# Reordering the first weight loads of a decode kernel by row length, and the query product with them

## The chip, the cores and the metric

One core of one Trainium2 chip. The time is the device time of one execution in microseconds; a kernel's time is the median of several runs. The span in a profile is the part between the first and the last instruction, some 2 us less. PE, DVE, ACT, POOL and SP are the core's TensorE, VectorE, ScalarE, GpSimd and SyncE; "PEclk" is the TensorE clock that was granted. A load runs on 16 DMA engines at once, and a row is one contiguous run of a load for one partition: the piece that one DMA engine moves in one record.

## The reference, cut to what matters

```python
# x: (8, 1, 448) bf16;  k_cache, v_cache: (8, 8, 4096, 256), the last W = 1024 positions are used
# wq: (448, 4096);  wo: (4096, 448);  w1: (448, 1792);  w2: (1792, 448)
q = (x @ wq).reshape(B, Sq, 16, 256).transpose(0, 2, 1, 3)
# k, v: the positions used, each head repeated for two heads of q
scores = einsum("bhqd,bhkd->bhqk", q, k) * 256 ** -0.5
a = einsum("bhqk,bhkd->bhqd", softmax(scores), v)...reshape(B, Sq, 4096) @ wo
b = gelu(layernorm(x) @ w1 + b1) @ w2 + b2
g = sigmoid((x * gate_w).sum(-1))
out = g * a + (1 - g) * b
```

Every weight and every cached key and value is read once: 77.7 MB for little arithmetic.

## The kernel before

All large inputs come through one stream of loads on one queue (SP), into a ring of nine slots of 16 KB per partition. `pump` issues loads as long as slots are free; `done` frees one. A `rows_loader` issues one load per piece, and a piece's row length is the length of one contiguous run per partition. The 448 rows of wq are three blocks of 128 (r = 0, 1, 2) and a tail of 64, cut into two halves so that it fills 128 partitions.

```python
wq_m = A_wq[0:DM, :].rearrange("(p r) n -> p (r n)", r=NR)          # 128 x 12288, HD = 4096
wq_t = A_wq[DM:D, :].rearrange("r (h n) -> (r h) n", h=2)           # 128 x 2048
add(("wq", 0), rows_loader([wq_m[:, 0 : 2 * HD]]))                  # 16 KB rows
add(("wq", 1), rows_loader([wq_m[:, 2 * HD : 3 * HD], wq_t]))       # 8 KB, then 4 KB rows
add_kv("k", A_k_cache, 0)                                           # 16 KB rows
add(("w1",), rows_loader([w1_m, w1_t]))
add(("w2",), rows_loader([w2_v]))
# ... keys and values in turn, then wo
pump()
nc.scalar.dma_start(x_sb[:], xf)          # four small loads on the ACT queue: x, gate, b2, b1
# ... gate_w broadcast, b2, b1
# ... constants; nc.gpsimd.memset(qw[:], 0.0), 4.4 us on POOL
def query():
    for r in range(NR + 1):
        w, o = slot("wq", r // 2), (r % 2) * HD
        for n in range(W // QN):
            for t in range(QUAD):
                # ... half, c: which half of the tail, which column
                nc.tensor.matmul(Sq[32 * t : 32 * t + NB, n * QN : (n + 1) * QN],
                                 lhsT=xT[:, r + half, :], rhs=w[:, o + c : o + c + QN],
                                 start=(r == 0), stop=(r == NR), skip_group_check=True)
    done(2)
# norm_and_gate(); query(); then keys, scores, values ...
```

## Time and profile before

| | before |
|---|---|
| time, median of 3 runs (lowest to highest) | 190.34 us (189.83 to 190.40) |
| span of the profiled run | 188.2 us |
| HBM read | 77.68 MB, 413 GB/s over the span |
| stream's rate between 24 and 180 us | 430 GB/s |
| PE / DVE / ACT busy | 70% / 67% / 24% |

No engine is at its limit, but the load stream is. So what counts is when the stream begins to flow, whether it ever pauses, and when the last of its 16 DMA engines is done.

### The profile page before, as it was taken

Reading aid. Unit: us, or ns where it says so; the run is one execution under the profiler, and the core shown is the slowest. Engines: PE = TensorE matmul, PEld = TensorE weight load, DVE = VectorE, ACT = ScalarE, POOL = GpSimd, SP = SyncE. Lnnn points to the kernel's source line nnn. Section 1 sums busy time; section 2 is a strip of 40 time slices with the busy share of each in tenths; the row PEclk is TensorE's granted clock in tenths of the full one; section 3 lists DMA queues with packets and bytes.
Section 4 is the critical chain, followed back from the end, with each engine's and each line's share of the span. In section 5 each row is a group of like instructions: output and inputs, shape, how many; then the busy total and the mean of one; then the engine's idle time right before and its main releaser. Section 6 shows DMA issues by size and latency. Waiting matters only on the chain.

```text
span 188.2 us, 2351 instructions
## 1 busy us (share of the span) xinstructions
PE 132.2 (70%) x938; PEld 68.0 (36%) x950; DVE 126.7 (67%) x177; ACT 45.4 (24%) x93; POOL 6.7 (4%) x15
## 2 busy tenths in 40 slices
PE   0017969998857986666957597849385969698974
PEld 0012853344425342422433153324142424245452
DVE  3960478999949494949494949595867767695300
ACT  3032310134040404040404031404040313125300
POOL 8500000000000000000000000000000000000000
PEclk9999756999997599996999789999999999999999
DMA  6999999999999999999999999999999999999991
GB/s 210 417 435 428 436 425 426 432 432 432 428 428 435 428 435 428 428 432 428 432 437 425 421 439 435 421 432 439 425 425 435 439 428 425 425 442 432 409 392 38
DMA packets 6396, 77.83 MB, mean 413 GB/s; under 512 B 857, under 2 KB 1138, under 8 KB 1778
## 3 DMA queue, kind: packets, MB, share of 16 engines
q1 hardware_dynamic: 6208, 77.67, 97.1%
q8 instruction: 7, 0.11, 0.2%
q10 hardware_dynamic: 178, 0.02, 0.1%
q14 instruction: 3, 0.02, 0.0%
HBM read 77.68 MB, written 0.01 MB: 413 GB/s over the span
## 4 chain that ended last, share of the span: by engine, by line
DMA 76%; DVE 15%; PE 4%; ACT 2%; issue 1%; DVEq 0%; ACTq 0%; SPq 0%
DMA slot<-in_A_k_cache_dram 40%; DMA slot<-in_A_v_cache_dram 20%; DMA slot<-in_A_wo_dram 15%; DVE kt L344 7%; DMA x_sb<-in_A_x_dram 2%; PE Sq L358 2%; DVE xz L243 1%; ACT qw L399 1%; DVE mx L428 1%; DVE qw L401 1%; ACT qs L368 1%; PE A_lo L662 0%; PE qp L386 0%; PE qt L373 0%; DVE ET L458 0%
## 5 line engine op out<-in xcount | busy, mean ns | idle before, releaser
L344 DVE STREAM_TRANSPOSE kt<-slot 128x2048 int32<-128x2048 int32 x32 | 73.7, 2306 | 31.8 <-DMA slot<-in_A_k_cache_dram 31.8
L416 PE MATMUL S<-kt,qw 128*128 128x512 bf16 x256 | 66.0, 402 | 31.0 <-DVE kt L344 28.5
L416 PEld LDWEIGHTS <-qw 128*128 128x128 bf16 x256 | 25.6, 100 | 66.3 <-issue 43.9
L521 ACT ACTIVATE oT<-fin,gg_s 128x16 bf16<-128x16 f32 x16 | 5.2, 328 | 75.0 <-PE fin L518 75.0
L445 ACT ACTIVATE E<-S,nmx 128x1024 bf16<-128x1024 f32 x16 | 22.2, 1389 | 1.9 <-DVE nmx L442 1.9
L428 DVE TENSOR_REDUCE mx<-S 128x1 f32<-128x1024 f32 x16 | 19.0, 1186 | 0.0
L488 PE MATMUL PO<-slot,ET 128*16 128x512 bf16 x256 | 17.5, 395 | 0.3 <-DMA slot<-in_A_v_cache_dram 0.3
L497 ACT ACTIVATE first<-PO,own 128x256 f32<-128x256 f32 x16 | 7.6, 474 | 27.0 <-PE PO L488 27.0
L458 DVE STREAM_TRANSPOSE ET<-E 128x512 int32<-128x512 int32 x16 | 11.2, 698 | 2.2 <-ACT E L445 2.2
L436 PE MATMUL mz<-m,same 128*128 128x4 f32 x32 | 6.2, 265 | 5.7 <-ACT oT L521 5.4
L410 PE MATMUL S<-place,foreign 128*128 128x512 bf16 x25 | 9.8, 390 | 0.1
L436 PEld LDWEIGHTS mz<-m,same 128*128 128x128 f32 x32 | 5.0, 195 | 7.5 <-ACT oT L521 6.6
L469 PEld LDWEIGHTS den<-rowsum,rowden 128*128 128x128 f32 x32 | 6.4, 206 | 3.1 <-issue 0.8
L488 PEld LDWEIGHTS <-ET 128*16 128x16 bf16 x256 | 5.1, 89 | 4.9 <-issue 1.0
L410 PEld LDWEIGHTS <-foreign 128*128 128x128 bf16 x32 | 3.2, 99 | 8.6 <-issue 6.9
L480 ACT ACTIVATE rsel<-sel,rb 128x8 f32<-128x8 f32 x16 | 4.7, 292 | 1.0 <-DVE rb L479 1.0
L469 PE MATMUL den<-rowsum,rowden 128*128 128x1 f32 x32 | 4.9, 222 | 0.0
L401 DVE CAST qw<-qp 32x512 bf16<-32x512 f32 x4 | 2.7, 686 | 3.1 <-ACT qw L399 3.1
L662 PE MATMUL A_lo<-slot,oP 128*8 128x224 bf16 x32 | 3.7, 258 | 1.2 <-DMA slot<-in_A_wo_dram 1.1
L290 POOL MEMSET qw<- 128x5120 bf16 x1 | 4.4, 4355 | 0.0
L593 PEld LDWEIGHTS <-foreign 128*128 128x128 bf16 x33 | 2.9, 99 | 3.6 <-issue 0.8
L593 PE MATMUL idle<-place,foreign 128*128 128x512 bf16 x16 | 4.1, 378 | 0.1
(144 smaller groups left out, 99.4 us busy)
## 6 DMA issues: line engine op xcount, KB each, us to landing
slot<-in_A_k_cache_dram SPq DMA_DIRECT2D x16, 2048.0 KB, 38.8
slot<-in_A_v_cache_dram SPq DMA_DIRECT2D x16, 2048.0 KB, 36.9
slot<-in_A_wo_dram SPq DMA_DIRECT2D x3, 896.0 KB, 30.9
slot<-in_A_wq_dram SPq DMA_DIRECT2D x1, 2048.0 KB, 7.5
slot<-in_B_w_dram SPq DMA_DIRECT2D x1, 1568.0 KB
slot<-in_B_w_dram SPq DMA_DIRECT2D x1, 1344.0 KB, 11.8
slot<-in_A_wq_dram SPq DMA_DIRECT2D x1, 1024.0 KB, 9.5
slot<-in_A_wo_dram SPq DMA_DIRECT2D x1, 672.0 KB, 27.7
```

What stands on the lines that cost most here:

```text
L344: nc.vector.transpose(kt[:].rearrange("p c k x r -> p (c k x r)").bitcast(WORD), kn[:, hf * CH * Dh : (hf + 1) * CH * Dh].bitcast(WORD),)
L410: nc.tensor.matmul(S[u][:, cols], lhsT=foreign[:], rhs=place[:], start=True, stop=False)
L416: nc.tensor.matmul(S[u][:, cols], lhsT=qw[:, j, u, m * RQ : m * RQ + P], rhs=kt[:, :, k, :, par], start=False, stop=(k == NK - 1 and par = ...
L428: nc.vector.reduce_max(mx[:], S[u][:], axis=AXIS.X)
L436: nc.tensor.matmul(mz[:], lhsT=same[:], rhs=m4[:], start=True, stop=True)
L445: nc.scalar.activation(E[:].rearrange("p c x i -> p c i x"), S.pop(u)[:].rearrange("p (c i x) -> p c i x", i=PAIR, x=BLK), ACT.Exp, bias=n ...
L458: nc.vector.transpose(ET[:].rearrange("p c r i -> p (c r i)").bitcast(WORD), E[:].rearrange("p c x i -> p (c x i)").bitcast(WORD),)
L469: nc.tensor.matmul(den[u][:], lhsT=rowden[:], rhs=rowsum[:], start=True, stop=True)
L488: nc.tensor.matmul(PO[32 * t : 32 * t + PAIR * RQ], lhsT=ET[:, c, 0:RQ, :], rhs=vn[:, PAIR * c * Dh : PAIR * (c + 1) * Dh], start=(c < QUA ...
L497: nc.scalar.activation(first[:], PO[:, 0, :], ACT.Copy, scale=own[:, 0:1])
L521: nc.scalar.activation(oT[:, half * RQ : (half + 1) * RQ, :, b].rearrange("p h j -> p j h"), sm[:], ACT.Copy, scale=gg_s[:, b : b + 1],)
L593: nc.tensor.matmul(dst, lhsT=foreign[:], rhs=place[:], start=True, stop=True)
```

## The change

Its intent is to begin the stream with short rows, so that the first data is through sooner, and to let the product take its row blocks in the order in which they land.

```diff
-    add(("wq", 0), rows_loader([wq_m[:, 0 : 2 * HD]]))
-    add(("wq", 1), rows_loader([wq_m[:, 2 * HD : 3 * HD], wq_t]))
+    add(("wq", 0), rows_loader([wq_t, wq_m[:, 0:HD]]))
+    add(("wq", 1), rows_loader([wq_m[:, HD : 3 * HD]]))
@@ query()
-        for r in range(NR + 1):
-            w, o = slot("wq", r // 2), (r % 2) * HD
+        for r in (NR, *range(NR)):
+            w = slot("wq", 0 if r in (NR, 0) else 1)
+            o = {NR: 0, 0: HH, 1: 0, 2: HD}[r]
@@ matmul
-                        start=(r == 0),
-                        stop=(r == NR),
+                        start=(r == NR),
+                        stop=(r == NR - 1),
```

(HH is 2048: the tail fills the first 2048 columns of the first slot, and block 0 follows.)

## The prediction

> **What bounds the kernel now.** I read the page's busy rows and its chain first, then the first microseconds of the DMA stream, the stretches of the run, the queue's waits and the timeline around the query product.
>
> The page, parts 2 and 4 (40 slices of 4.7 us; DMA in tenths, below it GB/s; then the chain's shares):
>
> ```profile
> DMA  6999999999999999999999999999999999999991
> GB/s 210 417 435 428 436 425 426 432 432 432 428 428 435 428 435 428 428 432 428 432 437 425 421 439 435 421 432 439 425 425 435 439 428 425 425 442 432 409 392 38
> HBM read 77.68 MB, written 0.01 MB: 413 GB/s over the span
> DMA 76%; DVE 15%; PE 4%; ACT 2%; issue 1%; DVEq 0%; ACTq 0%; SPq 0%
> ```
>
> The load stream is full from the second slice to the last but one, at about 430 GB/s. The engines have room (PE 70%, DVE 67%). The kernel is one queue of 77.7 MB, and its time is start of the stream, plus bytes over rate, plus a tail. The chain's end (start, length, what) fixes the tail:
>
> ```profile
> 119.99 36.94 DMA slot<-in_A_v_cache_dram
> 156.95 27.70 DMA slot<-in_A_wo_dram
> 184.65 0.04 issue
> ```
>
> The last load lands at 184.65, and the last products, two copies and the store bring the span to 188.2: 3.55 us that the change doesn't touch.
>
> The stretches of the run (us, then the engines' busy times, PE clock, DMA share, GB/s) show the beginning and the end of the stream:
>
> ```profile
> 1.50:2.00 0.50, 0.00 (x0) 0.00 (x0) 0.44 (x2) 0.50 (x1) 0.50 (x5) 1.00 1.78 360
> 2.00:2.50 0.50, 0.00 (x0) 0.00 (x0) 0.48 (x1) 0.22 (x2) 0.50 (x3) 1.00 0.55 98
> 2.50:3.00 0.50, 0.00 (x0) 0.00 (x0) 0.00 (x0) 0.00 (x0) 0.50 (x2) 1.00 0.24 100
> 3.00:3.50 0.50, 0.00 (x0) 0.00 (x0) 0.00 (x0) 0.00 (x0) 0.50 (x1) 1.00 1.00 406
> 24.00:180.00 156.00, 118.28 (x762) 58.72 (x774) 114.98 (x137) 39.06 (x83) 0.00 (x0) 0.93 1.01 430
> 183.00:184.00 1.00, 0.91 (x17) 0.69 (x17) 0.00 (x0) 0.00 (x0) 0.00 (x0) 1.00 0.58 233
> 184.00:185.00 1.00, 0.88 (x12) 0.45 (x12) 0.00 (x0) 0.00 (x0) 0.00 (x0) 1.00 0.21 81
> ```
>
> A record's bytes are booked where it starts, so the first rows, which are long, look like a burst and then a hole. The DMA records one by one tell it better. The first 16 rows, one to each of 16 engines and 16 KB each, start at 1.78 to 2.14 us (two of them at 2.58 and 2.72) and end between 2.91 and 3.60, 3.24 on average. Fourteen took 1.04 to 1.69 us, the two late ones 0.62 and 0.61, and any later 16 KB row takes 0.611. The excess of the first 16 is 0.63 us per engine. From there on no engine pauses. At the other end the share falls through 183 and 184: the engines don't finish together.
>
> The sum closes. Completions of successive 2 MB loads are 4.862 us apart, or 431 GB/s. After the first rows (0.26 of 77.67 MB) there are 77.41 MB, 179.5 us; 3.24 + 179.5 = 182.7 for the average engine. The last is 2.0 us later (184.7), since an instruction fetch of 16 KB holds up the one engine it falls on: the 16 completions of one load lie 0.53 us apart before the fetch at 24.4 us, and 1.77 us from then on.
>
> The SP queue's waits and the timeline round the query product:
>
> ```profile
> SPq L133 <- DMA slot<-in_A_wq_dram: 5.3, 1, 5.3
> 4.58 2.51 DVE L243 COPY xz<-x_sb 8x64 bf16<-8x64 bf16 x2 [2.10 <-DMA x_sb<-in_A_x_dram]
> 13.64 0.56 PE L333 MATMUL gp<-each 8*128 8x8 f32 x2 [1.63 <-DVE each L331]
> 14.13 3.51 PE L358 MATMUL Sq<-slot,xT 128*8 128x512 bf16 x32
> ```
>
> The fifth load (w1) isn't issued until the first (wq) has landed, at 8.23 us. The 32 query products begin right after the gate's little product, in program order on PE, without a wait for weights: the last of wq lands at 11.6 in the DMA records, 2.5 us before.
>
> **What the Trainium skill says.** "DMA: Bandwidth & Descriptors", section "Queues, rings and completion order", says that each DMA engine takes turns between the queues it has work for, a packet at a time. The trace agrees: x_sb's 896-byte rows, on the ACT queue, start at 2.90 to 3.49 us, each as a first 16 KB row ends. The same page, "Bandwidth" (its measured table), has the rate fall for small transfers. Within this stream the row length matters little: 4 KB rows take 0.159 us (412 GB/s over 16 engines), 8 KB rows 0.309 (424), 16 KB rows 0.611 (429). "Latency and other measured facts" on that page gives an HBM access 0.2 us on average and up to 2 us under load; the first rows' excess of 0.63 us lies between, but no view tells whether it is that. "PSUM — Partial Sum Buffer", "PSUM: the matmul accumulator", says that the first matmul of a group clears the written marks of its bank and quadrants and the rest accumulate. The diff moves start and stop with the order, so the product is the same sum in another order; no trace line bears on that.
>
> **The change part by part.**
> 1. Loads. The same 3.5 MB of wq in three loads before and after: 16, 8, 4 KB rows become 4, 8, 16 KB. No instruction and no byte is added or taken away. In the stream the cost is a sum over rows, 8 per engine of each kind (8 x 0.159 + 8 x 0.309 + 8 x 0.611 = 8.63 us), and doesn't depend on the order: 0.
> 2. The first rows. What changes is which rows meet the slow start. If the start is a fixed delay before data flows (0.63 us of it, then the line rate), the first 4 KB row ends earlier and the next follows: the same bytes by the same time, 0. If the excess is in proportion to the row (a long row has to be in before it goes out, which would be twice 0.61, close to the mean of 1.24 us), a quarter of it is left and 0.63 x 3/4 = 0.47 us is gained. If each engine gets just one row through before some point near 3 us, 12 KB less per engine is through by then, and 12/16 x 0.611 = 0.46 us is lost.
> 3. Issue. The first load is 512 KB instead of 2 MB. It lands after some 8 x 0.159 = 1.3 us of stream, at about 4 us instead of 7.9, so w1 is issued at about 4.2 instead of 8.23. The queue then holds more, but it held over 5 MB (some 13 us) at that moment already and never ran dry: 0.
> 4. x_sb. Its rows now wait for 4 KB rows instead of 16 KB ones, so it can land 0.4 to 0.9 us earlier than 4.48. But the two copies that follow (2.51 us for 8x64, where the like pair for y takes 0.29) end at 7.09, just after POOL's long memset at 7.01, and I expect them to end there again. The query product stays at 14.1, and if it came earlier, it is under the stream: 0.
> 5. The query product. 32 matmuls in another order, the same 3.5 us. Its last weights (16 KB rows now) land at 11.3 to 11.6, still 2.5 us ahead of PE: 0.
> Sum: 0, plus what the first rows do, between -0.47 and +0.46 us.
>
> **The rivals.** *The fixed delay* (nothing comes of it, 190.3): for it speaks that the two engines that began late took a normal 0.61 us and ended along with the others, as if all had waited for one moment. *The excess scales with the row* (189.9): for it speaks the factor of two, and that somebody made the change; against it the same two late engines. *The loss of one row's worth* (190.8): nothing speaks for it but that a start with short rows has less in flight. A fourth way is **the spread of the engines**: the end is set by the engine that an instruction fetch hit, and the order in which the engines begin (0.53 us apart) may fall otherwise, up to 0.3 us either way. That a new wait for weights appears in front of the query product would need 2.5 us, and even then the keys' slots are freed far ahead of the stream (a key load is issued at 38.31 and lands at 74.17).
>
> **Range and chances.** I give 0.5 to the fixed delay, 0.38 to the scaling, 0.12 to the loss: 0.38 x -0.47 + 0.12 x 0.46 = -0.12 us, so 190.2 us. The range takes the scaled gain with 0.2 us of spread at one end (189.5) and the loss with less at the other (190.8); the runs of the kernel before already lie 0.57 apart. Two per cent are 3.8 us, more than all that happens before the stream's first data: within 2% has 0.98.
>
> **What would show it.** Right: DMA share and GB/s as before from the second slice on; w1 issued near 4.2; the query product at 14.1 with no wait for a slot; wo landing within 0.5 us of 184.65. Which case it is, the average end of the first MB or so tells: level with before (fixed), 0.4 to 0.5 earlier (scaled) or later (loss). Wrong: a hole in the DMA share after 3 us, a rate of the first 3.5 MB off 8.6 us by more than 0.2, or the query product behind a wait for weights.

## The result, and the profile after

The changed kernel took 190.31 us (190.25 to 190.32, 4 runs) beside 190.22 us (189.83 to 190.40, 4 runs) of the kernel before: a ratio of 1.0007 with a 95% interval of 0.9990 to 1.0025. It is the same time. Ratios here are the mean time of one kernel's fast runs over that of the other's of the same rounds, so not quite the ratio of the medians quoted.

One kernel's runs lie some 0.5 us apart, about as far as the predicted cases lie from each other, so the time alone can't tell these apart; the traces have to.

The page after (parts 2 and 4: DMA busy tenths, GB/s, HBM total, the chain's shares):

```profile
DMA  5999999999999999999999999999999999999991
GB/s 205 411 438 416 426 434 430 428 431 435 428 424 435 438 428 424 431 435 431 424 433 435 428 424 435 431 435 424 431 431 431 428 435 431 428 424 435 413 394 42
HBM read 77.68 MB, written 0.01 MB: 412 GB/s over the span
DMA 76%; DVE 16%; PE 4%; ACT 2%; issue 1%; DVEq 0%; ACTq 0%; SPq 0%
```

The same picture: first slice 205 instead of 210 GB/s, full stream behind it. The end of the chain (start, length, what) after:

```profile
120.44 36.86 DMA slot<-in_A_v_cache_dram
157.30 0.02 issue
157.32 27.52 DMA slot<-in_A_wo_dram
```

The last load lands at 157.32 + 27.52 = 184.84 us, 0.19 later than the 184.65 of before. The stretches after (busy times, PE clock, DMA share, GB/s; a record counts where it starts):

```profile
1.50:2.00 0.50, 0.00 (x0) 0.00 (x0) 0.45 (x2) 0.50 (x1) 0.50 (x5) 1.00 0.54 106
2.00:2.50 0.50, 0.00 (x0) 0.00 (x0) 0.48 (x1) 0.21 (x2) 0.50 (x3) 1.00 0.67 221
2.50:3.00 0.50, 0.00 (x0) 0.00 (x0) 0.00 (x0) 0.00 (x0) 0.50 (x2) 1.00 0.75 216
3.00:3.50 0.50, 0.00 (x0) 0.00 (x0) 0.00 (x0) 0.00 (x0) 0.50 (x1) 1.00 1.09 372
24.00:180.00 156.00, 119.25 (x753) 58.79 (x765) 115.25 (x137) 38.97 (x83) 0.00 (x0) 0.92 1.01 430
```

The middle of the run is as before, 430 GB/s. The start isn't: with short rows a record is booked near where it runs, so the 216 GB/s at 2.5 to 3 us are real. This half microsecond is where the story lies. The queue and the product after (waits: engine, line, for whom, total, times, longest; then the timeline):

```profile
SPq L133 <- DMA slot<-in_A_wq_dram: 3.6, 2, 1.9
4.02 3.08 DVE L243 COPY xz<-x_sb 8x64 bf16<-8x64 bf16 x2 [1.54 <-DMA x_sb<-in_A_x_dram]
4.72 2.85 SPq L133 DMA_DIRECT2D slot<-in_B_w_dram  x3
13.65 0.56 PE L333 MATMUL gp<-each 8*128 8x8 f32 x2 [1.62 <-DVE each L331]
14.14 3.58 PE L359 MATMUL Sq<-slot,xT 128*8 128x512 bf16 x32
```

x lands 0.52 us earlier (3.96 instead of 4.48), its copies stretch from 2.51 to 3.08 us and end at 7.10 as before, w1 is issued at 4.72 instead of 8.23, and the product begins at 14.14 instead of 14.13.

**Looking closer at the start.** For the first microseconds I took the trace's DMA records one by one, spread each row's bytes evenly over its time and cut records at the edges of a stretch. "Occupied" below is the mean share of the 16 DMA engines that have a record running, those of small loads included (it can come out a little over 1, as records overlap slightly); "excess" is what rows took over the usual time of their length (0.159, 0.309, 0.611 us for 4, 8, 16 KB), summed and divided by 16.

| trace | first row ends (mean) | occupied 2.5 to 3 us | 0.5 MB through at | 1 MB | 4 MB | excess, 4 to 12 us |
|---|---|---|---|---|---|---|
| before | 3.24 us | 0.96 | 3.84 us | 5.02 us | 12.11 us | 0.00 us |
| after | 2.22 us | 0.63 | 3.78 us | 5.04 us | 12.33 us | 0.26 us |

The short rows do what they were meant to do: an engine's first row is through a whole microsecond earlier. Then, over half a microsecond, a third of the engines on average have nothing running. 1 MB is through at the same time as before, and later, while rows of 8 and 16 KB run, many take longer than usual, which puts the stream 0.2 us behind.

The hole has a sharp form. From some 2.4 to 2.8 us on, only about eight engines run rows of the stream (8.2 on average), for 0.3 to 0.6 us. This is so in each of the five traces below that have short rows and load x at once. x has eight rows of 896 bytes. In three of the five the eight others stand idle before the first row of x begins (in the second trace of the changed kernel from 2.62 us, with x's rows from 2.90). So they aren't busy with x: it looks as if each waited for its one row of x. The records don't name their engine, so that last step isn't shown.

### The profile page after: what moved, and what is told of

Same layout as the page of the kernel before. It is cut to its first block, busy times and chain, and to the rows that moved or that the text cites. A ratio compares the mean times of both kernels' runs of the same rounds, so it can differ in the third digit from the quotient of the medians.

```text
span 188.4 us, 2351 instructions
## 1 busy us (share of the span) xinstructions
PE 133.6 (71%) x938; PEld 68.4 (36%) x950; DVE 127.5 (68%) x177; ACT 45.4 (24%) x93; POOL 6.7 (4%) x15
## 4 chain that ended last, share of the span: by engine, by line
DMA 76%; DVE 16%; PE 4%; ACT 2%; issue 1%; DVEq 0%; ACTq 0%; SPq 0%
DMA slot<-in_A_k_cache_dram 40%; DMA slot<-in_A_v_cache_dram 20%; DMA slot<-in_A_wo_dram 15%; DVE kt L344 7%; PE Sq L359 2%; DVE xz L243 2%; DMA x_sb<-in_A_x_dram 2%; ACT qw L400 1%; DVE mx L429 1%; DVE qw L402 1%; ACT qs L369 1%; PE A_lo L663 0%; PE qp L387 0%; PE qt L374 0%; DVE ET L459 0%
## 5 line engine op out<-in xcount | busy, mean ns | idle before, releaser
L417 PE MATMUL S<-kt,qw 128*128 128x512 bf16 x256 | 67.4, 408 | 30.0 <-DVE kt L344 27.7
L443 DVE TENSOR_REDUCE nmx<-mz 128x1 f32<-128x4 f32 x16 | 2.3, 146 | 3.8 <-PE mz L437 3.7
```

The costliest lines, as they stand in the source:

```text
L417: nc.tensor.matmul(S[u][:, cols], lhsT=qw[:, j, u, m * RQ : m * RQ + P], rhs=kt[:, :, k, :, par], start=False, stop=(k == NK - 1 and par = ...
```

## The experiments

**A null, and the change again.** Both kernels unchanged, five rounds each, for the noise and for second traces.

> The kernel before, unchanged, as a null and for a second trace of the start. Time ratio 1.000 within 0.2%. If the slow start of the first 16 rows is a property of the kernel, it is there again: 14 of 16 rows over 1 us, none slow after 4 us, about 3.96 MB of the stream through at 12 us. If it is chance of the one trace, the number at 12 us moves by 0.1 MB or more.

> The changed kernel again. Theory A (short rows get data through earlier but the engines then run short between 2.5 and 3.2 us, and rows of 3.5 to 10 us are slower than usual): again a DMA share near 0.5 to 0.7 there, about 3.86 MB through at 12 us, last load 0.2 to 0.3 us later than in the kernel before, ratio 1.001. Theory B (chance of one trace): the bytes at 12 us lie within 0.03 MB of those of the kernel before and the slow rows between 4 and 10 us are gone; ratio 1.000.

The kernel before against itself: 190.36 us (189.92 to 190.45), ratio 1.0001 (0.9990 to 1.0013). The changed kernel again: 190.40 us (190.00 to 190.48), ratio 1.0006 (0.9993 to 1.0018). One kernel's runs lie 0.5 us apart, so a difference of 0.1 us can't be had from times. The traces are steadier. The null's reads 0.99 occupied at 2.5 to 3 us, 1 MB at 5.03, 4 MB at 12.12, no excess; the change's 0.62, 4.98, 12.26 and 0.25 us. The hole's line of the second trace:

```profile
2.50:3.00 0.50, 0.00 (x0) 0.00 (x0) 0.00 (x0) 0.00 (x0) 0.50 (x2) 1.00 0.56 214
```

The early row, the hole and the slow rows belong to the kernel and aren't chance (theory A). One part of theory A failed: the last load was to land 0.2 to 0.3 us later than in the kernel before, and in this pair it landed 0.1 us earlier (184.68 against 184.78 us).

**Which half of the change.** `loads_only` takes the new loads with the product's old order, `order_only` the old loads with the new order.

```diff
 # loads_only, against the changed kernel
-        for r in (NR, *range(NR)):
+        for r in range(NR + 1):
-                        start=(r == NR),
-                        stop=(r == NR - 1),
+                        start=(r == 0),
+                        stop=(r == NR),
 # order_only, against the kernel before
-        for r in range(NR + 1):
+        for r in (NR, *range(NR)):
-                        start=(r == 0),
-                        stop=(r == NR),
+                        start=(r == NR),
+                        stop=(r == NR - 1),
```

> The new order of the loads with the product in its old order. Both theories: as the changed kernel within 0.1%, with the query product at 14.1 us. If the order of the product mattered, this would differ from the changed kernel by over 0.15%.

> The old loads with the product taking the tail first. The tail lands at 11.6 us and the product starts at 14.1, so no wait: as the kernel before within 0.1%, query product at 14.1 us, and the start of the stream as in the kernel before.

`loads_only`: 190.30 us, ratio 1.0004 (0.9992 to 1.0016); `order_only`: 190.48 us, ratio 1.0008 (0.9996 to 1.0020). The product starts at 14.14 and 14.13 us. The start of the stream goes with the loads alone: 0.68 occupied, 4 MB at 12.14 us and 0.22 us excess in the first, 1.00, 12.11 and 0.01 in the second. The order of the product does nothing that shows. Until the product begins, `loads_only` is the same program as the changed kernel, so its start is a third trace of it: the lag at 4 MB is then 0.22, 0.14 and 0.03 us, which is how far it scatters.

**Where the rows lie in HBM.** In the change the 16 KB rows come from blocks 1 and 2 instead of 0 and 1. Here the kernel before reads them from there, in its old order of lengths.

```diff
-    add(("wq", 0), rows_loader([wq_m[:, 0 : 2 * HD]]))
-    add(("wq", 1), rows_loader([wq_m[:, 2 * HD : 3 * HD], wq_t]))
+    add(("wq", 0), rows_loader([wq_m[:, HD : 3 * HD]]))
+    add(("wq", 1), rows_loader([wq_m[:, 0:HD], wq_t]))
@@ query()
-            w, o = slot("wq", r // 2), (r % 2) * HD
+            w = slot("wq", 1 if r in (NR, 0) else 0)
+            o = {NR: HD, 0: 0, 1: 0, 2: HD}[r]
```

> The kernel before with its 16 KB rows taken from the second and third row blocks of wq (as in the changed kernel) and its 8 KB rows from the first; the order 16, 8, 4 KB stays. If where the 16 KB rows lie in HBM makes them slow, an excess of 100 ns or more per engine shows after 4 us (0 to 7 in the three traces of the old order). If the order of lengths does, it stays under 20 ns, with first rows at 1.2 to 1.3 us and 3.95 MB through at 12 us. Time within 0.3%.

190.26 us, ratio 1.0004 (0.9989 to 1.0019); 0.98 occupied, 4 MB at 12.12 us, excess 0.01 us. The place of the rows isn't it.

**When w1 and the rest are issued.** In the change the fifth load is issued at 4.72 us instead of 8.23. Here the changed kernel's first pump stops after three slots, and the rest is issued after POOL's long memset.

```diff
-        while len(slots) < min(len(plan), consumed[0] + RING):
+        while len(slots) < min(len(plan), consumed[0] + depth[0]):   # depth = [3] at first
+    def w1_late(t):
+        nc.gpsimd.memset(t[:, 0:16], 0.0)
+        rows_loader([w1_m, w1_t])(t)
-    add(("w1",), rows_loader([w1_m, w1_t]))
+    add(("w1",), w1_late)
     nc.gpsimd.memset(qw[:], 0.0)
+    depth[0] = RING
+    pump()
```

> The changed kernel with the loads of w1 and all behind it issued not from 4.3 us on but after POOL's long memset, near 7.3 us and later. If the early issue is what slows rows between 4 and 12 us, the excess there falls from 217 to 256 ns per engine to under 100 and what is left lies after 7 us, and 3.93 MB or more is through at 12 us. If the cause is the rows themselves or the small loads, it stays at 200 or more. Time within 0.3%.

w1 is issued at 7.16 us. 190.47 us, ratio 1.0015 (0.9999 to 1.0031); 0.64 occupied, 4 MB at 12.28 us, excess 0.18 us. It fell from 0.25 but not under 0.1: the early issue isn't the cause, or not most of it.

**The small loads, first try.** The four small loads of the ACT queue were moved behind POOL's long memset, in both kernels. To make ACT wait I gave it two new tiles of 4 bytes per partition to copy. The memset ends 0.87 us earlier in this place, so the small loads are issued from 6.21 us on.

```diff
-    nc.scalar.dma_start(x_sb[:], xf)     # and gate, b2, b1
+    flag = consts.tile([NB, 1], F32)
+    flag2 = consts.tile([NB, 1], F32)
+    nc.gpsimd.memset(qw[:], 0.0)         # moved up: runs at 1.78 us on POOL instead of 2.65
+    nc.gpsimd.memset(flag[:], 0.0)
+    nc.scalar.copy(flag2[:], flag[:])
+    nc.scalar.dma_start(x_sb[:], xf)     # and gate, b2, b1
```

> The changed kernel with the four small loads of the ACT queue (x, gate, biases) issued only after POOL's long memset, near 7 us, so that nothing but the 4 KB and 8 KB rows is in the stream before. If the hole at 2.5 to 3 us (share 0.62 to 0.68 in three traces) comes from those small loads taking turns, the share there goes to 0.95 or more and 0.66 MB or more is through at 4 us (0.59 to 0.65 now). If it comes from the supply of row descriptors of the stream itself, the share stays at 0.7 or less. The slow rows of 4 to 12 us (217 to 256 ns in excess per engine) should go below 50 ns if b1's 28-byte packets cause them. The query product starts near 17 us; time within 0.3%.

> The same edit to the kernel before. If the small loads cause the slow first 16 KB rows (1.22 to 1.29 us on average instead of 0.61), these fall to under 0.8 us and the bytes through at 4 us rise from 0.56 to over 0.60 MB. If the slow start is the stream's own, first rows stay over 1.1 us. Time within 0.3%.

The start answered: 1.02 occupied at 2.5 to 3 us in the changed kernel, while the first rows of the kernel before still took 1.23 us. But both kernels came out slower, 191.33 us (ratio 1.0060, 1.0043 to 1.0078) and 191.77 us (1.0084, 1.0067 to 1.0100), which no theory of the start allowed for. The DMA records have each 2 MB load 4.894 to 4.895 us after the one before it, for the whole run, where all runs so far have 4.862. Loads that end before 18 us hardly do that at 100 us. The edit's own tiles may: they are allocated before the slots and push them up in their partition, by 64 bytes as I count it (no view shows addresses). So I tried the shift by itself and the edit without it.

**The slots' address.** The kernel before with its padding tile 64 bytes longer.

```diff
-    consts.tile([P, 112], BF16, name="pad")
+    consts.tile([P, 144], BF16, name="pad")
```

> The kernel before with its padding tile 64 bytes longer, so that all slots start 64 bytes later in each partition, and nothing else. If the slots' address caused the slower loads of the two shifted runs, each 2 MB load takes 4.893 to 4.899 us and the time is 0.5 to 0.7% up (32 such loads and the rest by 0.033 us per 2 MB: about 1.2 us). If it was the late small loads, 4.862 us and ratio 1.000.

191.56 us, ratio 1.0075 (1.0062 to 1.0088), 4.894 us per 2 MB load. The stretch of the shifted kernel that answers to the one of before:

```profile
24.00:180.00 156.00, 122.69 (x742) 59.78 (x752) 115.14 (x137) 38.68 (x82) 0.00 (x0) 0.89 1.01 427
```

427 instead of 430 GB/s, or 0.7%, and the time is 1.40 us up, a little more than the 1.2 expected. It is the stream's own rows that slow down: between 30 and 150 us a 16 KB row takes 0.6157 us on average instead of 0.6119. Everything behind the padding tile moved, not the slots alone, but no other tile is written by these rows. The first two small-loads runs have the same slow rows (0.6159 us) and aren't used for times.

**The small loads, second try.** The same without new tiles: ACT copies a piece of the memset tile into `rstd`, which is overwritten later anyway. No tile is added, so slots are back at their address.

```diff
-    nc.scalar.dma_start(x_sb[:], xf)     # and gate, b2, b1
+    nc.gpsimd.memset(qw[:], 0.0)         # moved up as before
+    nc.scalar.copy(rstd[:], qw[0:NB, 0, 0, 0:1])
+    nc.scalar.dma_start(x_sb[:], xf)     # and gate, b2, b1
```

> The same edit as the first late-small-loads run of the changed kernel, but without the two new tiles that had shifted the slots by 64 bytes. If the shift caused the 0.6% there, each 2 MB load takes 4.862 us again (4.893 to 4.899 with the shift). Start as there: share 0.95 or more at 2.5 to 3 us, 0.66 MB or more through at 4 us and 4.0 MB or more at 12 us. If the hole was what ate the gain of the short rows, the last load lands 0.1 to 0.3 us before that of the same edit on the kernel before; ratio 0.9975 to 1.000. If an engine's fetch of instructions sets the end whatever the start, no difference is seen beyond the noise of 0.15%.

> The same on the kernel before: first rows still over 1.1 us, 0.56 MB through at 4 us and 3.95 MB at 12 us, 4.862 us per 2 MB load, ratio 0.999 to 1.001.

Stretches of the changed kernel with late small loads:

```profile
2.50:3.00 0.50, 0.00 (x0) 0.00 (x0) 0.00 (x0) 0.00 (x0) 0.50 (x1) 1.00 0.99 385
3.00:3.50 0.50, 0.00 (x0) 0.00 (x0) 0.00 (x0) 0.00 (x0) 0.50 (x1) 1.00 1.01 401
```

Where the changed kernel moved 216 GB/s there are 385: the hole is gone. 1 MB is through at 4.72 us, 0.31 us before the same edit of the kernel before (5.03), and 4 MB at 11.88 against 12.12. The shifted pair above says the same of 1 MB (4.72 against 5.02). The first rows of the kernel before are still slow without any small load beside them (1.09 us). Each 2 MB load takes 4.862 us in both.

The times don't follow. The changed kernel took 190.44 us (189.94 to 190.62), ratio 1.0013 (1.0000 to 1.0026), the kernel before 190.24 us (189.98 to 190.60), ratio 1.0004 (0.9992 to 1.0016). The profiled run of the former was its fastest (189.94); the other four have no trace. So the 0.2 to 0.3 us at the head of the stream are seen in the traces of two pairs (in this one the last load also lands 0.23 us earlier, 184.33 against 184.56), and aren't shown in the time. It was the candidate for a kernel faster than both, and it isn't one. (The product begins at 18.84 us there instead of 14.14 at no visible cost in its profiled run.)

**x alone.** As before, but x is loaded at once and only the gate and the biases are late.

```diff
     nc.scalar.dma_start(x_sb[:], xf)     # stays first
+    nc.gpsimd.memset(qw[:], 0.0)         # moved up in the text
+    nc.scalar.copy(rstd[:], qw[0:NB, 0, 0, 0:1])
     # gate, b2, b1 from here
```

> The changed kernel with x loaded at once and only the gate's and the biases' loads late. If it is the traffic of many small packets or the number of loads that makes the hole at 2.5 to 3 us, the share there is 0.9 or more and 0.66 MB or more is through at 4 us. If x's own eight rows on the second queue are enough to stall the stream, the share stays at 0.6 to 0.75. Query product at 14 to 15 us. Ratio 0.9975 to 1.001.

Its stretches:

```profile
2.50:3.00 0.50, 0.00 (x0) 0.00 (x0) 0.00 (x0) 0.00 (x0) 0.50 (x1) 1.00 0.71 258
3.00:3.50 0.50, 0.00 (x0) 0.00 (x0) 0.00 (x0) 0.00 (x0) 0.50 (x1) 1.00 0.92 296
```

The hole is back, only a little later: 258 and 296 GB/s, 0.77 occupied at 2.5 to 3 us (a little above what I had allowed for x alone) and 0.90 at 3 to 3.5, with 1 MB through at 5.12 us. Loading x at the start is enough. Their records take 0.24 us on average there, 0.22 in the first trace of the changed kernel and 0.06 in the second (with the same hole), against 0.04 in the kernel before: so it isn't only the time of the records themselves that is lost. Nor do such rows cost this at any time: the gate's load has eight rows of 896 bytes too, at 4.8 to 5.3 us in the changed kernel, and there 15.6 engines still run the stream; x's own rows, when late (10.2 us on), leave no hole either. Whether another first load on the ACT queue in x's place would make the hole was not tried. The time is 190.83 us, ratio 1.0029 (1.0017 to 1.0040), above what I had expected (up to 1.001), and the product begins at 13.60 us, not 14 to 15. The time is up by more than the some 0.28 us by which its stream lags at 28 us (below), and I have no cause for the rest.

**The ledger.** All traces with the slots in place; the last column is the mean moment at which the 16 engines complete the eighth load (the second keys' 2 MB), near 28.7 us.

| rows | trace | occupied 2.5 to 3 | 1 MB at | 4 MB at | excess 4 to 12 us | eighth load |
|---|---|---|---|---|---|---|
| 16, 8, 4 KB | before | 0.96 | 5.02 | 12.11 | 0.00 | 28.65 |
| | before again | 0.99 | 5.03 | 12.12 | 0.00 | 28.67 |
| | order only | 1.00 | 5.01 | 12.11 | 0.01 | 28.67 |
| | other rows | 0.98 | 5.03 | 12.12 | 0.01 | 28.67 |
| | small loads late | 0.83 | 5.03 | 12.12 | 0.00 | 28.66 |
| 4, 8, 16 KB | after | 0.63 | 5.04 | 12.33 | 0.26 | 28.88 |
| | after again | 0.62 | 4.98 | 12.26 | 0.25 | 28.81 |
| | loads only | 0.68 | 4.90 | 12.14 | 0.22 | 28.71 |
| | late issue | 0.64 | 5.05 | 12.28 | 0.18 | 28.85 |
| | x early, three late | 0.77 | 5.12 | 12.23 | 0.15 | 28.94 |
| | small loads late | 1.02 | 4.72 | 11.88 | 0.11 | 28.47 |

The first three traces of the new order are at 28.80 on average, the first four of the old at 28.66: the change costs the average engine 0.14 us. That would be 0.07%, which is just what the two ratios (1.0007, 1.0006) say, and neither can be told from 1. Behind that, from the eighth load to the last row of wo, these eleven traces take from 156.07 us (again) to 156.65 us (order only). The end's own scatter of 0.6 us is larger than anything that the start does.

## Why the prediction was right or wrong

The time was right: 190.31 us against 190.2, within 189.5 to 190.8, within 2%. By its steps:

- *What bounds it* held. From 3.5 us on the 16 engines are occupied in every run, and a shift by 64 bytes, which took the stream from 430 to 427 GB/s, moved the time more than everything else here.
- *Part 1, the loads' order costs 0*: nearly, though one of its signs of being wrong did come. From the mean end of the first rows to 3.5 MB the changed kernel takes 9.3 us (2.22 to 11.56) where the sum of its rows gives 8.47; the kernel before takes 8.1 where the sum gives 8.02. The hole of part 4 and the slow rows make up the difference. (That the queue's 5 MB are some 13 us was a slip: at 431 GB/s they are 12. Nothing hangs on it.) The rows aren't quite a sum that ignores the order: those of 4 to 12 us took 0.22 to 0.26 us per engine more than usual behind a start with short rows, and nothing more behind one with long rows. That is a term of 0.2 us that the sum lacked. It isn't the rows' place in HBM, for the old order with the new addresses has none. It isn't mainly the early issue (0.18 left). With late small loads 0.11 is left, and 0.17 in the shifted run: these may be a part of it, not all. What it is stays open. One observation: the excess of all rows up to 12 us is 0.62 to 0.72 us per engine in the first four traces of the old order and 0.44 to 0.66 us in the first three of the new, as if a cost of starting were paid either by the first rows or in portions. That is argued, not shown.
- *Part 2, the first rows*: the favoured case, the fixed delay, is wrong. First 4 KB rows end at 2.22 us on average, where a fixed 0.63 us from the mean start of 1.90 plus their 0.16 would be 2.7, and in the six other traces with short rows first they end at 2.14 to 2.41. The loss of a row's worth is wrong too. With the small loads out of the way, 0.31 us of the 0.47 that the scaled case promised are there at 1 MB: the excess does shrink with the row to a large part (the first 4 KB rows took 0.09 to 0.30 us more than usual in the seven traces, the first 16 KB rows 0.48 to 0.68 in the other seven). I had held the two late engines against it, which was reading too much from two of sixteen.
- *Part 3, the issue*: right in kind. w1 was issued at 4.72 and 4.42 us in the two traces, not 4.2, because the first load meets the hole (4.28 in the shifted run without one).
- *Part 4, x*: right for x and its copies (0.52 us earlier, end at 7.10, product at 14.14), and **the step that failed for the stream**. I counted x's earlier landing as free. With short rows in front of it, eight of the 16 engines go without a row of the stream for 0.3 to 0.6 us about the time that x's eight rows come in. Late small loads remove the hole, x alone brings it back. So what went wrong is this zero, worth about 0.3 us at 1 MB, and it hid a gain of the same size in part 2. Two errors cancelled, and the total looked like the fixed delay: that the time came out right was in part luck. What keeps these engines from their next row isn't to be seen in these traces.
- *Part 5, the product*: right: 14.14 us, 3.58 us long, no wait, and the order alone does nothing.
- *The spread of the engines*, given as up to 0.3 us either way, held: from the eighth load to the end the eleven traces lie within 0.58 us.

## What to carry to other kernels

When a stream of loads sets the time, a change at its head is worth at most the head's own loss (here some 0.6 us of 190), and a small load that comes in among its first rows can eat it (later ones did not here): check whether DMA engines go idle between the first rows, not only when the first row ends. An experiment that adds a tile moves everything allocated behind it; keep the addresses of the large buffers, or you measure the shift. And a time that comes out as predicted doesn't prove the steps: here a gain and a loss cancelled.

## What the Trainium skill lacked or had wrong

- "DMA: Bandwidth & Descriptors", "How a descriptor splits into AXI transactions", tells of descriptors that start off a 256-byte boundary and speaks of what is read. No page has a cost for the address in SBUF that a load writes: 64 bytes of shift took each 2 MB load (16 KB rows) from 4.862 to 4.894 us and the kernel 0.75% up.
- The same page, "Queues, rings and completion order", has the engines take turns by the packet; it doesn't say that a small load at the start can cost far more than its packets' turn. With x's eight rows of 896 bytes among the first 4 KB rows, eight of the 16 engines ran no row of the stream for 0.3 to 0.6 us (0.63 occupied at 2.5 to 3 us); without them 1.02 were occupied, and 1 MB was through 0.3 us earlier.
- The same page, "Bandwidth", has no word on the first row of each engine in a stream, and what the page says elsewhere of a first byte isn't given by row length: first 16 KB rows took 1.09 to 1.29 us on average in seven traces (0.611 later), first 4 KB rows 0.24 to 0.46 us in the other seven (0.159 later).
- "Runtime: NRT & Kernel Launch", "Instruction fetch mechanics", says that instructions come in blocks of 16 KiB through the sequencer's own DMA queue. The trace agrees (seven packets of 16,384 bytes on the instruction queue), but the page calls the cost of a fetch mostly hidden. It speaks of the sequencer; the stream isn't spared: with the first fetch in the trace of before, at 24.4 us, the spread of the 16 engines' completions goes from 0.53 to 1.77 us, and the last engine ends the stream.
